# Part of the second-layer weights loaded from GpSimd's queue, in a one-core decode block

## The chip, the cores and the metric

The kernel runs on one core of a Trainium2 chip. The metric is the device time of one execution in microseconds (us), as a median of several runs. Five engines work beside each other: PE (TensorE, matmuls), DVE (VectorE), ACT (ScalarE), POOL (GpSimd) and SP (SyncE, which here only issues loads and the final store). Loads are carried by 16 DMA engines that all queues share.

## The reference

Two sequences (B = 2) of one token each pass an attention block with a cache and a dense block, both behind a layer norm. All data is float32.

```python
B, Sq, D = 2, 1, 512          # H, Sk, Dh = 32, 8192, 128 ; F = 1792
q = (layernorm(x) @ wq).reshape(B, Sq, H, Dh)
scores = einsum("bhqd,bhkd->bhqk", q, k_cache) * Dh ** -0.5
o = einsum("bhqk,bhkd->bhqd", softmax(scores), v_cache)
h = x + o.reshape(B, Sq, H * Dh) @ wo
r = relu(layernorm(h) @ w1 + b1)
out = h + (r * r) @ w2 + b2
```

The two caches are 64 pairs (head, sequence) of 4 MB of keys and 4 MB of values, 537 MB in all; the weights make up the rest of 561 MB.

## The kernel before

SBUF holds a ring of three slots of 64 KB per partition, `ring[0]` to `ring[2]`. One slot takes one pair: keys in its first half, values in its second. SP issues one load of 128 rows x 64 KB per pair (`load`, L127) whenever DVE has told it through the semaphore FREE that a slot is done; the loads run ahead of the work by up to two slots.

For each pair PE multiplies the keys with the query (L243), DVE takes the maximum (L249), ACT the exponential and its sum (L253), and DVE multiplies the values with the weights and sums (L258). Partial maxima, sums and products are kept and folded at the end.

The last pair is split up so that the end overlaps with its loads, and the slots are filled with the weights of the following layers. SP issues, in this order: the last keys (`kld`, slot 0), the first 24 heads of the output projection (`wod`, slot 1), the last values in three pieces (`vld`), the other 8 heads of `wod`, and, when slot 2 is free, the first-layer weights in two pieces (`w1d`) and the second-layer weights in four pieces (`w2d`, blocks 8, 4, 1 and 1 of the 14 blocks of 512 columns). Each load has a semaphore of its own that rises by 16 when all its parts have landed.

The compute at the end follows the same order. PE runs the output projection (L338) as its weights arrive, ACT and DVE form the second layer norm, PE multiplies with the first-layer weights (L386), DVE transposes, scales, adds the bias and squares the positive part (L396 to L403), and PE multiplies with the second-layer weights block by block (L410), waiting for each piece by `p.take(pe, LW2[k], 16)`. DVE copies the result (L415) and SP stores it (L417). Each block of L410 takes four matmuls in the code, which the trace shows as eight.

GpSimd builds an identity matrix at the start (L163, L165) and has nothing to do after that. The helper `p.take(engine, sem, n)` (L62) waits until a semaphore has reached n and takes n off again.

Of the kernel before, what the change touches and what calls it, by code (L numbers as in the profile page):

```python
# [17 lines left out]
FB = F // P  # L18
# [5 lines left out]
ROW = 2 * HALF  # L24
NG = BH - B
HG = H - 1
W2_PIECES = [8, 4, 1, 1]
W1_PIECES = [2, 2]
V_PIECES = [(0, 3), (3, 6), (6, 8)]
HA = 24  # L30
# [34 lines left out]
def attention_block_kernel(nc, small, kvd, wqd, kld, vld, wod, w1d, w2d, out):  # L65
    p = Program(nc)
    pe, dve, act, pool, sp = nc.tensor, nc.vector, nc.scalar, nc.gpsimd, nc.sync
# [52 lines left out]
    LV = [p.sem(f"v63_{k}") for k in range(len(V_PIECES))]  # L120
    LW1 = [p.sem(f"w1_{k}") for k in range(len(W1_PIECES))]
    LW2 = [p.sem(f"w2_{k}") for k in range(len(W2_PIECES))]
    FREE, SCORES, MAXED, EXPED, BUFFER, QUERY = (p.sem(n) for n in ("free", "scores", "maxed", "exped", "buffer", "query"))
    OUT = nc.alloc_semaphore("out")

    def load(tile, src, sem):
        sp.dma_start(tile, src).then_inc(sem, 16)  # L127

    W1 = ring[2][:, : DB * F].rearrange("p (d f) -> p d f", f=F)
    W2 = ring[2][:, DB * F : DB * F + FB * D].rearrange("p (m c) -> p m c", c=D)  # L130
# [19 lines left out]
        load(ring[0][:, HALF + a * CS : HALF + b * CS], vld[:, a * CS : b * CS], LV[k])  # L150
    load(WO[:, HA:], wod[:, HA:], LO)
    p.take(sp, FREE)
    at = 0
    for k, n in enumerate(W1_PIECES):
        load(W1[:, at : at + n], w1d[:, at : at + n], LW1[k])
        at += n
    at = 0
    for k, n in enumerate(W2_PIECES):
        load(W2[:, at : at + n], w2d[:, at : at + n], LW2[k])
        at += n  # L160
# [3 lines left out]
    p.after("pool", t_id)  # L164
    t_id = p.tell("pool", pool.affine_select(out=ident, in_=ident, compare_op=ALU.not_equal, fill=1.0, base=0,  # L165
                                             pattern=[[-1, P]], channel_multiplier=1))
    dve.memset(ones_d, 1.0 / D)
    dve.memset(eps_t, EPS)
    dve.memset(zero, 0.0)
# [232 lines left out]
    p.after("dve", tok)  # L402
    tok = p.tell("dve", dve.scalar_tensor_tensor(a2, a1, 0.0, a1, op0=ALU.max, op1=ALU.mult))  # L403
    p.after("pe", tok)
    at_m = 0
    for k, n in enumerate(W2_PIECES):
        p.take(pe, LW2[k], 16)
        for m in range(at_m, at_m + n):
            for j in range(NQ):
                ins = pe.matmul(o[32 * j : 32 * j + B, :], a2[:, m, :], W2[:, m, j * P : (j + 1) * P],  # L410
                                start=False, stop=(m == FB - 1))
        at_m += n
# [39 lines left out]
```

## Time and profile before

| | us |
|---|---|
| median of 3 runs | 1303.91 |
| lowest, highest | 1303.83, 1304.21 |
| the profiled execution's own time | 1303.67 |
| its span in the profile | 1301.9 |
| busy: PE, DVE, ACT, POOL | 412.5, 757.7, 160.1, 0.7 |

The profile comes from one execution. Its span runs from the first instruction to the end of the last one or of the last transfer; the 1.8 us beside it lie outside what the profile shows. A row of the timeline gives the start, the length, the engine, the line, the operation and its tiles, the count, and in brackets the idle time before it with the instruction that ended it. SPq and POOLq are the instruction queues of these engines. A row of the issues gives the tile and its source, the queue, the size and the time from issue to landing. The mean granted TensorE clock of this run was 0.637 of full speed.

### The profile page before, as it was taken

Reading aid. Unit: us, or ns where it says so; the run is one execution under the profiler, and the core shown is the slowest. Engines: PE = TensorE matmul, PEld = TensorE weight load, DVE = VectorE, ACT = ScalarE, POOL = GpSimd, SP = SyncE. Lnnn points to the kernel's source line nnn. Section 1 sums busy time; section 2 is a strip of 40 time slices with the busy share of each in tenths; the row PEclk is TensorE's granted clock in tenths of the full one; section 3 lists DMA queues with packets and bytes.
Section 4 is the critical chain, followed back from the end, with each engine's and each line's share of the span. In section 5 each row is a group of like instructions: output and inputs, shape, how many; then the busy total and the mean of one; then the engine's idle time right before and its main releaser. Section 6 shows DMA issues by size and latency. Waiting matters only on the chain. (4 is left out here: it accounts for less than half of the span.)

```text
span 1301.9 us, 8206 instructions
## 1 busy us (share of the span) xinstructions
PE 412.5 (32%) x2372; PEld 109.2 (8%) x2372; DVE 757.7 (58%) x1221; ACT 160.1 (12%) x267; POOL 0.7 (0%) x6
## 2 busy tenths in 40 slices
PE   1323223223323313323323323322322332331346
PEld 0100000000000000000000000000000000000012
DVE  1465575575565565566566466557557556556664
ACT  0011011011011011111111111101101101101120
POOL 0000000000000000000000000000000000000000
PEclk9766566666566566656656566656656666656668
DMA  9999999999999999999999999999999999999998
GB/s 419 419 448 423 445 423 447 423 441 429 421 449 421 447 423 445 423 447 423 443 427 423 447 421 447 423 447 421 447 423 445 425 429 441 421 447 423 447 412 368
DMA packets 11236, 561.13 MB, mean 431 GB/s; under 512 B 1376, under 2 KB 1504, under 8 KB 1760
## 3 DMA queue, kind: packets, MB, share of 16 engines
q1 hardware_dynamic: 11088, 561.06, 99.7%
q8 instruction: 3, 0.05, 0.0%
q10 hardware_dynamic: 144, 0.01, 0.0%
q14 instruction: 1, 0.01, 0.0%
HBM read 561.00 MB, written 0.07 MB: 431 GB/s over the span
## 5 line engine op out<-in xcount | busy, mean ns | idle before, releaser
L243 PE MATMUL s<-ring,qc 128*32 128x512 f32 x2048 | 376.8, 903 | 845.2 <-PEq L62 845.2
L258 DVE SCALAR_TENSOR_TENSOR ring<-ring,s 128x1024 f32<-128x1024 f32 x512 | 589.2, 1217 | 0.2 <-DVEq L62 0.2
L249 DVE TENSOR_REDUCE nm<-s 128x1024 f32 (+1 forms) x128 | 156.7, 1225 | 488.6 <-DVEq L62 488.6
L253 ACT ACTIVATE s<-s,nm 128x1024 f32<-128x1024 f32 x128 | 139.3, 1088 | 1081.6 <-ACTq L62 1081.6
L243 PEld LDWEIGHTS s<-ring,qc 128*32 128x32 f32 x2048 | 94.1, 157 | 1128.0 <-issue 1128.0
L258 DVE DVE_READ_ACCUMULATOR ring<-ring,s (+1 forms) x512 | 42.9, 84 | 0.0
L253 ACT ACTIVATION_READ_ACCUMULATOR s<-s,nm (+1 forms) x128 | 24.7, 193 | 0.0
L200 DVE TENSOR_REDUCE part<-sm 128x2 f32<-128x8 f32 x1 | 0.2, 161 | 19.4 <-DVEq L62 19.4
L338 PE MATMUL pm<-ring,big 128*32 128x512 f32 x64 | 10.7, 828 | 2.2 <-issue 1.4
L220 PE MATMUL s<-ring,xr 128*32 128x512 f32 x64 | 9.6, 770 | 2.3 <-issue 2.3
L202 PE MATMUL pm<-part,ones_d 128*128 128x2 f32 x2 | 0.6, 364 | 23.5 <-DVE part L200 23.5
L225 DVE STREAM_TRANSPOSE big<-s 128x512 f32<-128x512 f32 x2 | 1.4, 717 | 9.1 <-PE s L220 9.1
L274 DVE COPY qc<-qs 128x96 f32 x21 | 5.1, 243 | 0.0
L386 PE MATMUL s<-ring,xr 128*32 128x448 f32 x32 | 4.8, 726 | 0.5 <-issue 0.5
L193 ACT ACT_TABLE_LOAD x1 | 1.3, 1283 | 25.4 <-PE pm L191 25.4
L410 PE MATMUL s<-ring,a 128*2 128x128 f32 x112 | 3.5, 272 | 2.6 <-PEq L62 2.6
L372 DVE TENSOR_TENSOR hc<-xc,pm 128x8 f32<-128x8 f32 x1 | 0.2, 164 | 6.0 <-PE pm L366 6.0
L195 DVE RECIPROCAL rstd<-rstd 128x2 f32<-128x2 f32 x2 | 0.3, 166 | 5.5 <-ACT rstd L193 5.5
L220 PEld LDWEIGHTS s<-ring,xr 128*32 128x32 f32 x64 | 2.6, 137 | 8.4 <-issue 8.4
L338 PEld LDWEIGHTS pm<-ring,big 128*32 128x32 f32 x64 | 2.6, 143 | 8.2 <-issue 8.2
L297 PE MATMUL pm<-nm,pick 128*128 128x128 f32 x8 | 2.1, 441 | 3.7 <-DVE xb L290 3.7
L415 DVE COPY res<-s 128x128 f32<-128x128 f32 x1 | 0.3, 292 | 5.0 <-PE s L410 5.0
(62 smaller groups left out, 31.2 us busy)
## 6 DMA issues: line engine op xcount, KB each, us to landing
ring<-in_wod SPq DMA_DIRECT2D x1, 6144.0 KB, 27.3
ring<-in_kld SPq DMA_DIRECT2D x1, 4096.0 KB, 31.0
ring<-in_w1d SPq DMA_DIRECT2D x2, 1792.0 KB, 28.2
ring<-in_vld SPq DMA_DIRECT2D x2, 1536.0 KB, 32.2
ring<-in_wod SPq DMA_DIRECT2D x1, 2048.0 KB, 40.2
ring<-in_w2d SPq DMA_DIRECT2D x1, 2048.0 KB, 34.6
ring<-in_vld SPq DMA_DIRECT2D x1, 1024.0 KB, 35.8
ring<-in_w2d SPq DMA_DIRECT2D x1, 1024.0 KB, 36.7
```

Of the source, the lines that this page charges most:

```text
L193: tok = p.tell("act", act.activation(rstd, bank[:, :B], AF.Sqrt, bias=eps_t, scale=1.0))
L220: ins = pe.matmul(s[0][32 * j : 32 * j + 32, n * 512 : n * 512 + 512], xs[:, d, :], ring[2][:, c0 : c0 + 512], start=(d == 0), stop=(d == ...
L225: tok = p.tell("dve", dve.transpose(big[:, n * 512 : n * 512 + 512], s[0][:, n * 512 : n * 512 + 512]))
L243: ins = pe.matmul(s[k][32 * j : 32 * j + 32, n * 512 : (n + 1) * 512], qc[:, u, :], slot[:, c0 : c0 + 512], start=True, stop=True)
L249: dve.tensor_reduce(at(nm, pair, NC, c, 1), s[k], axis=AX.X, op=ALU.max, negate=True).then_inc(MAXED, 1)
L253: act.activation(s[k], s[k], AF.Exp, bias=at(nm, pair, NC, c, 1), scale=1.0, accum_out=at(ls, pair, NC, c, 1)).then_inc(EXPED, 1)
L258: return dve.scalar_tensor_tensor(v, v, 1.0, s[k], op0=ALU.mult, op1=ALU.mult, accum_out=at(ac, pair, NC * NH, c * NH + e, 1))
L274: dve.tensor_copy(qc, qs[:, bass.ds(i + 3, 3)][:, :, None].to_broadcast([P, 3, 32])).then_inc(QUERY, 1)
L297: ins = pe.matmul(pm[0][:, j * BH * NC : (j + 1) * BH * NC], pick[:, j, :], nm, start=True, stop=True)
L338: ins = pe.matmul(pm[1][32 * j : 32 * j + 32, :], big[:, h * 32 : h * 32 + 32], WO[:, h, :], start=(h < NQ), stop=(h + NQ >= H))
L386: ins = pe.matmul(y[32 * j : 32 * j + 32, :], xs[:, d, :], W1[:, d, j * FQ : (j + 1) * FQ], start=(d == 0), stop=(d == DB - 1))
L410: ins = pe.matmul(o[32 * j : 32 * j + B, :], a2[:, m, :], W2[:, m, j * P : (j + 1) * P], start=False, stop=(m == FB - 1))
```

## The change

The first two of the 14 blocks of `w2d` (4 KB in each of 128 partitions, 512 KB) are no longer part of SP's first second-layer load, which shrinks from 8 blocks to 6. GpSimd loads them in four loads that split the partitions into 12, 2, 98 and 16 rows. SP tells GpSimd through a new semaphore GO that slot 2 is free, right before it issues the first-layer weights. GpSimd waits for its four loads, resets its own record of DMA semaphores (`dma_reset`) and raises FIRST. PE waits for FIRST ahead of the first second-layer matmul.

```diff
-W2_PIECES = [8, 4, 1, 1]
+W2_PIECES = [6, 4, 1, 1]
+W2_FIRST = FB - sum(W2_PIECES)
+W2_ROWS = [12, 2, 98, 16]
...
     p.take(sp, FREE)
+    sp.sem_inc(GO, 1)
     at = 0
     for k, n in enumerate(W1_PIECES):
         load(W1[:, at : at + n], w1d[:, at : at + n], LW1[k])
         at += n
-    at = 0
+    at = W2_FIRST
     for k, n in enumerate(W2_PIECES):
         load(W2[:, at : at + n], w2d[:, at : at + n], LW2[k])
         at += n
...
+    p.take(pool, GO)
+    at = 0
+    for n, sem in zip(W2_ROWS, LW2F):
+        pool.dma_start(W2[at : at + n, :W2_FIRST], w2d[at : at + n, :W2_FIRST]).then_inc(sem, 16)
+        at += n
+    for sem in LW2F:
+        pool.wait_ge(sem, 16)
+    pool.dma_reset()
+    pool.sem_inc(FIRST, 1)
...
     p.after("pe", tok)
+    p.take(pe, FIRST)
     at_m = 0
     for k, n in enumerate(W2_PIECES):
         p.take(pe, LW2[k], 16)
+        n += W2_FIRST * (k == 0)
         for m in range(at_m, at_m + n):
```

More of the change, by code (lines that the diff above doesn't have):

```diff
@@ L122, in attention_block_kernel @@
     LW2 = [p.sem(f"w2_{k}") for k in range(len(W2_PIECES))]
+    LW2F = [p.sem(f"w2_rows_{k}") for k in range(len(W2_ROWS))]
+    GO, FIRST = p.sem("slot2"), p.sem("w2_first")
     FREE, SCORES, MAXED, EXPED, BUFFER, QUERY = (p.sem(n) for n in ("free", "scores", "maxed", "exped", "buffer", "query"))
```

## The prediction

> **What bounds the kernel now.** I read the page's head, its queue part and the stretches first, to see whether any engine sets the time.
>
> ```profile
> span 1301.9 us, 8206 instructions
> q1 hardware_dynamic: 11088, 561.06, 99.7%
> HBM read 561.00 MB, written 0.07 MB: 431 GB/s over the span
> ...
> 120.00:1200.00 1080.00, 330.51 (x1792) 82.46 (x1792) 649.86 (x1024) 134.91 (x224) 0.00 (x0) 0.62 1.00 434
> ```
>
> The first column group of the last row is the stretch, then busy us of PE, PEld, DVE, ACT and POOL, the granted TensorE clock, the share of the 16 DMA engines and GB/s. Through the body the DMA share is 1.00 at 434 GB/s, and DVE, the busiest engine, has work for 650 of 1080 us. The kernel is bound by its loads. 434 GB/s over 16 engines is 27.1 GB/s each, so a row of 4096 bytes (two blocks of 512 floats, what the change moves per partition) takes one engine 4096 / 27,100 = 0.151 us. Bytes are the same before and after, so nothing can come from the body; what is left is how the loads end. Next the end, in quarters of a microsecond:
>
> ```profile
> 1296.50:1297.00 0.50, 0.50 (x28) 0.50 (x20) 0.00 (x0) 0.00 (x0) 0.00 (x0) 1.00 0.98 369
> 1297.00:1297.25 0.25, 0.25 (x17) 0.25 (x12) 0.00 (x0) 0.00 (x0) 0.00 (x0) 1.00 1.04 393
> 1297.25:1297.50 0.25, 0.25 (x20) 0.22 (x8) 0.00 (x0) 0.00 (x0) 0.00 (x0) 1.00 0.57 213
> 1297.50:1297.75 0.25, 0.25 (x12) 0.00 (x0) 0.00 (x0) 0.00 (x0) 0.00 (x0) 1.00 0.50 148
> 1297.75:1298.00 0.25, 0.01 (x2) 0.00 (x0) 0.00 (x0) 0.00 (x0) 0.00 (x0) 1.00 0.23 90
> 1298.00:1298.25 0.25, 0.00 (x0) 0.00 (x0) 0.00 (x0) 0.00 (x0) 0.00 (x0) 1.00 0.19 74
> 1298.25:1298.50 0.25, 0.15 (x8) 0.18 (x12) 0.00 (x0) 0.00 (x0) 0.00 (x0) 1.00 0.13 49
> 1298.50:1298.75 0.25, 0.25 (x16) 0.25 (x12) 0.00 (x0) 0.00 (x0) 0.00 (x0) 1.00 0.13 49
> 1298.75:1299.00 0.25, 0.25 (x16) 0.25 (x12) 0.00 (x0) 0.00 (x0) 0.00 (x0) 1.00 0.11 41
> 1299.00:1299.25 0.25, 0.25 (x20) 0.25 (x13) 0.00 (x0) 0.00 (x0) 0.00 (x0) 1.00 0.00 0
> ```
>
> This is the view that matters. A share of 0.13 is two engines of 16. All sixteen are busy until 1297.25; about twelve run dry around 1297.4; one more by 1298.0 (0.23 is under four), a third laggard by about 1298.25 (0.19 is three), and the last two work alone from 1298.25 to 1299.0. Every load of 128 rows is dealt over all engines, so each of its semaphores waits for the last of them. From 1297.25 on the column of GB/s gives (213+148+90+74+49+49+41) x 0.25 = 166 KB, which sixteen engines would move in 0.38 us: perfect balance would end the loads at 1297.63 instead of 1299.0. **So 1.4 us is the most that any redistribution can gain**, about 0.1% of the time.
>
> Why there are laggards: instruction packets of 16 KB go through single DMA engines beside the loads.
>
> ```profile
> q8 instruction: 2, 0.03, 0.3%
> ```
>
> That is the queue row of 1250 to 1302 us: two such packets, 0.6 us of one engine each at 27.1 GB/s. Whoever carries one is late for good, since its queue of loads never runs empty to catch up.
>
> Last, what PE does with the loads at the end:
>
> ```profile
> 1282.36 3.45 PE L338 MATMUL pm<-ring,big 128*32 128x512 f32 x16 [0.87 <-PEq L62]
> 1288.36 2.75 PE L386 MATMUL s<-ring,xr 128*32 128x448 f32 x16 [0.48 <-issue]
> 1291.56 2.06 PE L386 MATMUL s<-ring,xr 128*32 128x448 f32 x16
> 1294.82 0.19 DVE L403 SCALAR_TENSOR_TENSOR a<-a 128x28 f32<-128x28 f32 x1
> 1295.83 1.93 PE L410 MATMUL s<-ring,a 128*2 128x128 f32 x64 [2.00 <-PEq L62]
> 1298.35 1.62 PE L410 MATMUL s<-ring,a 128*2 128x128 f32 x48 [0.59 <-PEq L62]
> 1299.54 0.14 PEld L410 LDWEIGHTS s<-ring,a 128*2 128x2 f32 x8 [0.21 <-issue]
> 1300.04 0.29 DVE L415 COPY res<-s 128x128 f32<-128x128 f32 x1 [5.03 <-PE s L410]
> 1300.35 0.34 SPq L417 DMA_DIRECT2D out<-res  x1
> ...
> 1242.01 0.43 SPq L127 DMA_DIRECT2D ring<-in_wod  x1
> 1260.23 0.80 SPq L127 DMA_DIRECT2D ring<-in_w1d  x2
> 1261.08 8.84 SPq L127 DMA_DIRECT2D ring<-in_w2d  x4
> ...
> ring<-in_w1d SPq DMA_DIRECT2D x2, 1792.0 KB, 28.2
> ring<-in_wod SPq DMA_DIRECT2D x1, 2048.0 KB, 40.2
> ring<-in_w2d SPq DMA_DIRECT2D x1, 2048.0 KB, 34.6
> ```
>
> The second-layer matmuls (L410) stop and start with the loads: the activations are ready when L403 ends at 1295.01, but PE starts at 1295.83, since the first eight blocks land at 1261.1 + 34.6 = 1295.7; it stops again at 1297.76 for the next four, and the last eight weight loads begin at 1299.54, 0.54 after the last data packet. The copy, the store and the end follow at fixed distances. The other boundary is 1282.36: L338 starts right behind the second part of the output projection's weights, 1242.0 + 40.2 = 1282.2, and from there to L403 the chain is latency of compute.
>
> **The change, part by part.** Removed from SP: nothing but bytes, 8 blocks become 6 in one load; the four issues remain. Added to SP: one increment ahead of the first-layer loads; SP's next row is an issue that lands 28 us later, so it costs nothing. Added to PE: one wait (FIRST) ahead of L410, beside a wait that is 0.8 us longer; nothing but those matmuls is queued behind it. Added to POOL: a wait, four issues, four waits, a reset, an increment. POOL has nothing behind them and nobody waits for it except through FIRST.
>
> *When the rows land.* GpSimd's DMA issues are not in this trace. The nearest rows for a second queue beside SP's are those of the start:
>
> ```profile
> sm<-in_small ACTq DMA_DIRECT2D x1, 13.0 KB, 22.4
> ring<-in_wqd SPq DMA_DIRECT2D x1, 22.2
> ```
>
> 13 KB took as long as the load of 64 KB rows issued beside it: 8 small rows per engine took turns, one for one, with 8 big ones of 2.4 us (65,536 / 27,100). So here 9 or 10 rows take turns with what SP has queued when POOL is told, at 1260.23: rows of 48 KB (1.8 us) at worst. Ten rounds and four semaphore packets of 1.8 us end by 1286 with an issue time near SP's 0.4; on rows of 8 to 16 KB (0.3 to 0.6 us), which follow soon, nearer 1273. Both lie ahead of 1295.0, so FIRST is expected open, for nothing. The cover is 9 us in the worse case and over 20 in the likelier.
>
> *What they delay.* The moved rows come ahead of loads that were queued before them. An engine that carries 8 of them is 1.21 us later with the projection's weights, one with 9 is 1.36, one that is spared 0.15. From the first-layer loads' end on, the moved bytes are missing from SP's first second-layer load and the schedule is back.
>
> *Who carries what.* Eight rows per engine before. 12 + 2 + 98 + 16 is dealt anew: 98 is 14 x 7, so two engines get none of it, which saves them up to 7 x 0.151 = 1.06 us against eight rows, if one row of the 16 is left to them. With shares of one row for the 12, the 2 and the 16, counted from the first engine each time, the loads are 10, 10, ten times 9, 8, 8, 1, 1. The trace doesn't number the engines. Between the ends (the spared two are the last two: -1.06 for them; they are not: +0.15 to +0.30) I take the first, narrowly, because there are exactly two engines far behind. The Trainium skill, "DMA: Bandwidth & Descriptors", section on why a DMA increments its semaphore by 16, gives both dealings: k engines with k dividing the rows, from a cursor that moves on, or, for some direct copies from GpSimd, shares rounded up over all sixteen. By the second the two spared are the last-numbered; by the first the spared two depend on the cursor and get 2 rows, and 0.15 us less is saved. No run here shows which it is.
>
> *The sum, if the last two are spared.* Their end goes from 1299.0 to 1297.94. The twelve go from about 1297.4 to 1297.7 at most. What is late next is the third laggard, at 1298.25 with eight rows, unchanged. So the loads end 0.75 us earlier. PE must follow: the projection's weights now wait for that third engine, which was 0.75 ahead and is 1.21 later, +0.46; L403 ends at 1295.5 and L410 starts at 1295.6, its first piece having landed at 1295.7 - 0.75. Its 112 matmuls need 1.93 + 1.62 - 0.21 = 3.34 and would be through at 1298.9; the last piece, landing 0.75 earlier, lets the last eight weight loads begin at 1298.8 and the copy at 1299.3. Both agree, with little to spare. The copy comes 0.7 us earlier. The profiled execution took 1303.67, its span 1301.9 and 1.8 around it; the median of 1303.91 stands 0.24 above it. 1303.91 - 0.7 = **1303.2 us**.
>
> **The rivals.**
>
> *The spared engines are not the laggards.* Then the last two carry 9 or 10 rows and end 0.15 to 0.30 later; the projection's weights come 1.4 later, L403 ends at 1296.4, and PE's 3.34 us end at 1299.8, just inside. Copy at 1300.2 to 1300.3: 1303.91 + 0.2 = 1304.1 us. For it: 14 of 16 engines are not those two. Against it: nothing in the trace.
>
> *Nothing changes.* If GpSimd's queue deals 98 rows nearly evenly (98 / 16 is 6.1), or spares one laggard and not the other, the end stays: 1303.9 us. The Trainium skill, same page, section "Issuing engines are not separate DMA queues", speaks for this: all queues end on the same 16 engines, and issuing from several saves only issue time. By that rule the sum is 0. The body's 434 GB/s at a share of 1.00 agrees with it, but the quarters above show a loss that is balance and not rate.
>
> *The gate comes late (slower).* If GpSimd's rows queue behind what SP has already issued, they land with or after the last loads, and PE holds all 112 matmuls back at FIRST. PE then needs 3.34 us after the last landing where it now needs 0.5: 1303.91 + 2.9 = 1306.8 us. It decides from FIRST open later than about 1296.6 (1299.97 - 3.34), each microsecond costing one. For it: the backlog is 28 to 35 us at issue, as the times to landing say. Against it: the small load of the start, which took turns.
>
> **How the numbers follow.** Last two spared 0.50 (1303.2); others spared 0.30 (1304.1); nothing 0.09 (1303.9); gate late 0.06 (1306.8); 0.03 for another cost of the new queue that passes 2.6 us, 0.02 for a gain that passes it, which the 1.4 us above all but excludes. 0.2% of the time, 2.6 us, is about what a measurement of this kernel can tell from no change; the first three cases lie inside. Faster 0.02, same 0.89, slower 0.09. The range takes in the first three, with 0.4 below the first for a third laggard that also gains a little and 0.5 above the second for the issue costs not seen: 1302.8 to 1304.6.
>
> **What would show it.** Right: the DMA share falls from 1.0 to nothing within about 0.8 us instead of 1.75; L410 starts near 1295.6 and runs with hardly a stop; the copy comes 0.7 us earlier; POOL's rows land before 1286; L338's second start moves to about 1282.8. Wrong: two engines still alone for 0.75 us (others spared), L338's second start at 1283.6 (same), L410 waiting for FIRST past 1296.6 (gate late), or a span that is unchanged with a longer time around it.

## The result, and the profile after

The changed kernel takes 1307.59 us (13 runs, 1305.77 to 1308.08) where the kernel before takes 1303.91 (13 runs, 1303.65 to 1304.48). The ratio is 1.0025 with a 95% interval of 1.0017 to 1.0032: 3.7 us slower. The runs before lie in one group, those after in two, 1305.8 to 1306.2 and 1307.1 to 1308.1. The profiled execution of after took 1307.60, that of before 1303.67, so 3.93 us are to be explained between the two.

The page of after, and its issues and queue rows from 1250 us on. GpSimd's queue is q0.

```profile
span 1305.9 us, 8216 instructions
q1 hardware_dynamic: 11088, 560.53, 99.4%
q0 software_dynamic: 224, 0.52, 0.1%
...
ring<-in_w2d POOLq DMA_DIRECT2D x1, 392.0 KB, 13.0
ring<-in_w2d POOLq DMA_DIRECT2D x1, 64.0 KB, 13.5
ring<-in_w2d POOLq DMA_DIRECT2D x1, 48.0 KB, 7.5
ring<-in_w2d POOLq DMA_DIRECT2D x1, 8.0 KB, 7.4
ring<-in_wod SPq DMA_DIRECT2D x1, 2048.0 KB, 42.8
```

Rows from the end of the timeline of after (L131 issues a load, L175 GpSimd's, L272 is the product with the values, L352 the output projection, L417 the end of the activations, L426 the second-layer matmuls, L431 the copy).

```profile
1242.93 0.43 SPq L131 DMA_DIRECT2D ring<-in_wod  x1
1260.18 2.23 POOL L175 DMA_DIRECT2D ring<-in_w2d  x4 [1258.71 <-POOLq L64]
1274.33 1.22 DVE L272 SCALAR_TENSOR_TENSOR ring<-ring,s 128x1024 f32<-128x1024 f32 x1 [3.78 <-DVEq L64]
1283.06 1.22 DVE L272 SCALAR_TENSOR_TENSOR ring<-ring,s 128x1024 f32<-128x1024 f32 x1
1285.87 3.64 PE L352 MATMUL pm<-ring,big 128*32 128x512 f32 x16 [0.83 <-PEq L64]
1300.22 0.19 DVE L417 SCALAR_TENSOR_TENSOR a<-a 128x28 f32<-128x28 f32 x1
1300.66 3.24 PE L426 MATMUL s<-ring,a 128*2 128x128 f32 x112 [1.44 <-PEq L64]
1303.97 0.29 DVE L431 COPY res<-s 128x128 f32<-128x128 f32 x1 [3.56 <-PE s L426]
```

The two rows of before that answer to the products:

```profile
1271.30 1.22 DVE L258 SCALAR_TENSOR_TENSOR ring<-ring,s 128x1024 f32<-128x1024 f32 x1
1279.56 1.22 DVE L258 SCALAR_TENSOR_TENSOR ring<-ring,s 128x1024 f32<-128x1024 f32 x1
```

The gate does no harm: the rows land 7 to 14 us after their issues, by 1276. The loss begins with the values. DVE now waits 3.78 us for their first piece and starts at 1274.33 instead of 1271.30; its last product starts 3.50 later, and the second half of the projection 3.51 later (1282.36 to 1285.87). Its weights are as late as its products: they land at 1242.9 + 42.8 = 1285.7. From there to the end of the activations it takes 14.54 us instead of 12.65, another 1.89. Part comes back: PE waits 0.25 us instead of 0.82 for the second layer, and from its first matmul to the copy it takes 3.31 instead of 4.21, since no load stops it any more. 3.51 + 1.89 - 0.57 - 0.90 = 3.93.

Where the 3.5 us come from shows in the stretch in which GpSimd's rows move, 1264 to 1276 us. The last two columns are the DMA engines' busy share and GB/s. Before:

```profile
1264.00:1276.00 12.00, 7.24 (x45) 3.30 (x48) 8.49 (x14) 2.15 (x6) 0.00 (x0) 0.53 0.94 394
```

After:

```profile
1264.00:1276.00 12.00, 7.23 (x50) 2.76 (x53) 5.64 (x10) 1.96 (x4) 0.00 (x0) 0.58 0.92 306
```

The engines are nearly as busy (0.92 against 0.94) and move 22% less. (394 - 306) GB/s x 12 us is 1.06 MB, or 2.4 us of all sixteen at 434 GB/s. That is not a matter of who waits for whom but of rate.

And the end of the loads after, to be held against the quarters of the prediction:

```profile
1298.00:1298.50 0.50, 0.50 (x12) 0.16 (x8) 0.00 (x0) 0.00 (x0) 0.00 (x0) 1.00 0.98 393
1298.50:1299.00 0.50, 0.50 (x16) 0.15 (x8) 0.00 (x0) 0.00 (x0) 0.00 (x0) 1.00 0.89 344
1299.00:1299.25 0.25, 0.23 (x12) 0.00 (x0) 0.16 (x1) 0.00 (x0) 0.00 (x0) 1.00 0.95 369
1299.25:1299.50 0.25, 0.00 (x0) 0.00 (x0) 0.25 (x1) 0.00 (x0) 0.00 (x0) 1.00 0.98 385
1299.50:1299.75 0.25, 0.00 (x0) 0.00 (x0) 0.24 (x1) 0.00 (x0) 0.00 (x0) 1.00 0.67 254
...
1300.25:1300.50 0.25, 0.00 (x0) 0.00 (x0) 0.16 (x1) 0.00 (x0) 0.00 (x0) 1.00 0.19 74
1300.50:1300.75 0.25, 0.09 (x4) 0.12 (x8) 0.00 (x0) 0.00 (x0) 0.00 (x0) 1.00 0.19 74
1300.75:1301.00 0.25, 0.25 (x14) 0.24 (x15) 0.00 (x0) 0.00 (x0) 0.00 (x0) 1.00 0.17 66
1301.00:1301.25 0.25, 0.25 (x20) 0.25 (x12) 0.00 (x0) 0.00 (x0) 0.00 (x0) 1.00 0.07 25
1301.25:1301.50 0.25, 0.25 (x20) 0.25 (x12) 0.00 (x0) 0.00 (x0) 0.00 (x0) 1.00 0.02 8
```

About three engines (0.19, 0.17) still work alone from 1300.25 to 1301.0, and one (0.07, 0.02) until about 1301.3, where before two worked until 1299.0: the laggards are still there and the loads end 2.3 us later.

### The profile page after: what moved, and what is told of

The parts are those of the page before. It is cut to its first block, busy times and chain, and to the rows that moved or that the text cites. A ratio compares the mean times of both kernels' runs of the same rounds, so it can differ in the third digit from the quotient of the medians.

```text
span 1305.9 us, 8216 instructions
## 1 busy us (share of the span) xinstructions
PE 399.7 (31%) x2372; PEld 107.9 (8%) x2372; DVE 757.9 (58%) x1221; ACT 160.0 (12%) x267; POOL 2.9 (0%) x10
## 5 line engine op out<-in xcount | busy, mean ns | idle before, releaser
L257 PE MATMUL s<-ring,qc 128*32 128x512 f32 x2048 | 363.1, 873 | 858.6 <-PEq L64 858.6
L272 DVE SCALAR_TENSOR_TENSOR ring<-ring,s 128x1024 f32<-128x1024 f32 x512 | 589.3, 1217 | 4.4 <-DVEq L64 4.4
L272 DVE DVE_READ_ACCUMULATOR ring<-ring,s (+1 forms) x512 | 42.8, 84 | 0.0
L352 PE MATMUL pm<-ring,big 128*32 128x512 f32 x64 | 10.7, 824 | 2.2 <-issue 1.4
L175 POOL DMA_DIRECT2D ring<-in_w2d x4 | 2.2, 565 | 1258.7 <-POOLq L64 1258.7
L426 PE MATMUL s<-ring,a 128*2 128x128 f32 x112 | 3.2, 272 | 1.4 <-PEq L64 1.4
## 6 DMA issues: line engine op xcount, KB each, us to landing
ring<-in_wod SPq DMA_DIRECT2D x1, 2048.0 KB, 42.8
```

Source lines behind the costliest of these rows:

```text
L175: pool.dma_start(W2[at : at + n, :W2_FIRST], w2d[at : at + n, :W2_FIRST]).then_inc(sem, 16)
L257: ins = pe.matmul(s[k][32 * j : 32 * j + 32, n * 512 : (n + 1) * 512], qc[:, u, :], slot[:, c0 : c0 + 512], start=True, stop=True)
L272: return dve.scalar_tensor_tensor(v, v, 1.0, s[k], op0=ALU.mult, op1=ALU.mult, accum_out=at(ac, pair, NC * NH, c * NH + e, 1))
L352: ins = pe.matmul(pm[1][32 * j : 32 * j + 32, :], big[:, h * 32 : h * 32 + 32], WO[:, h, :], start=(h < NQ), stop=(h + NQ >= H))
```

## The experiments

My theory after reading the two traces was that the dealing of the rows costs the rate: a load of 128 rows gives each engine always the same partitions, while loads of 12, 2, 98 and 16 rows put partitions on engines that serve others (theory D). The rivals: the queue that GpSimd writes is slow for the engines (S), or any second queue beside SP's is (Q).

**e1, one load of 128 rows on GpSimd.**

```diff
-W2_ROWS = [12, 2, 98, 16]
+W2_ROWS = [128]
```

> Edit: GpSimd loads the same 512 KB in one load of 128 rows instead of 12, 2, 98 and 16. While GpSimd's rows moved in the changed kernel (1264 to 1274 us), the DMA engines were as busy as before but moved 300 to 340 GB/s where 418 to 430 was moved before. Theory D (the dealing: uneven shares put rows on engines that otherwise serve other partitions, and those transfers get in each other's way): with 128 rows dealt by eights the rate stays near 420, the first values (V, first piece) are awaited until about 1272 instead of 1274.3, the time is 1303.7 to 1304.5. Theory S (the software queue itself slows the engines): rate 300 to 340 again, time 1306 to 1308. Theory Q (any second queue): like S.

Measured: 1303.76 us (10 runs, 1303.43 to 1305.64), ratio to before 1.0001, 0.9991 to 1.0010. Its stretch, first product and second half of the projection:

```profile
1264.00:1276.00 12.00, 7.24 (x40) 3.52 (x42) 7.48 (x13) 2.65 (x6) 0.00 (x0) 0.50 0.93 387
...
1272.39 1.22 DVE L272 SCALAR_TENSOR_TENSOR ring<-ring,s 128x1024 f32<-128x1024 f32 x1 [0.62 <-DVEq L64]
1283.55 3.44 PE L352 MATMUL pm<-ring,big 128*32 128x512 f32 x16 [0.94 <-PEq L64]
```

The rate is back, on the same queue, for the same bytes at the same time. The moved bytes alone delay the first product by 1.09 us and the projection by 1.19; the median hides that, though three of the ten runs took 1305.4 to 1305.6. Theory S falls.

**e2 and e3, the same rows and the one load of 128 rows on ACT's queue.**

```diff
-    p.take(pool, GO)
...
+    p.take(act, GO)
+    r0 = 0
+    for n, sem in zip(W2_ROWS, LW2F):
+        act.dma_start(W2[r0 : r0 + n, :W2_FIRST], w2d[r0 : r0 + n, :W2_FIRST]).then_inc(sem, 16)
+        r0 += n
...
-    p.take(pe, FIRST)
+    for sem in LW2F:
+        p.take(pe, sem, 16)
```

> Edit: the four loads of 12, 2, 98 and 16 rows are issued by ACT, at the same signal from SP; PE waits for their four semaphores itself; nothing is left on GpSimd. Theory D: rate falls to 300 to 340 GB/s as in the changed kernel, time 1306 to 1308. Theory S: rate near 420 and time 1303.5 to 1304.5. Theory Q: like D.

> Edit: as the ACT kernel, but one load of 128 rows. Theory D and theory S: rate near 420, time 1303.5 to 1304.5. Theory Q (two queues taking turns cost a quarter of the rate, whoever issues): rate 300 to 340 and time 1306 to 1308.

Measured: e2 1308.37 us (7 runs, 1306.66 to 1310.06), ratio 1.0032, 1.0020 to 1.0043; e3 1303.93 (10 runs, 1303.61 to 1305.89), ratio 1.0004, 0.9995 to 1.0014. e2 lies 0.4 us above the 1306 to 1308 expected of it; why was not followed up. The stretch in e2:

```profile
1264.00:1276.00 12.00, 7.24 (x50) 2.71 (x52) 4.88 (x8) 1.96 (x4) 0.00 (x0) 0.58 0.90 309
...
q10 hardware_dynamic: 172, 0.52, 2.6%
```

In e3:

```profile
1264.00:1276.00 12.00, 8.07 (x56) 3.06 (x60) 6.72 (x12) 1.97 (x4) 0.00 (x0) 0.61 0.91 379
```

The loss goes with the rows and not with the queue: 309 GB/s with 12, 2, 98 and 16 rows, 379 with 128. Theory Q falls too.

**e4, GpSimd's rows signalled after all of SP's issues.**

```diff
-    sp.sem_inc(GO, 1)
...
     for k, n in enumerate(W2_PIECES):
         load(W2[:, at : at + n], w2d[:, at : at + n], LW2[k])
         at += n
+    sp.sem_inc(GO, 1)
```

> Edit: as the changed kernel, but SP signals GpSimd after its four second-layer issues (near 1270 us) instead of ahead of the first-layer issues (1259.6). GpSimd's rows then come among the first-layer weights and no longer among the last values. If the place does the harm (the values' first piece 3 us late, then the chain of products): DVE's products start by 1271.5 and end by 1281, and the time is set by the last load, 1303.5 to 1306.5 according to how much rate is lost there (up to 2.4 us). If the rate alone does it, wherever it falls: 1306 to 1308.

Measured: 1307.29 us (10 runs, 1305.85 to 1308.23), ratio 1.0024, 1.0014 to 1.0034, as slow as the changed kernel. Its rows:

```profile
1276.00:1280.00 4.00, 3.05 (x32) 0.67 (x20) 3.36 (x7) 0.00 (x0) 0.00 (x0) 1.00 1.01 338
1280.00:1284.00 4.00, 0.24 (x8) 0.16 (x8) 1.92 (x7) 0.00 (x0) 0.00 (x0) 0.83 1.06 325
...
1271.43 1.21 DVE L272 SCALAR_TENSOR_TENSOR ring<-ring,s 128x1024 f32<-128x1024 f32 x1
1286.24 3.52 PE L352 MATMUL pm<-ring,big 128*32 128x512 f32 x16 [4.14 <-PEq L64]
```

The values are on time now, at 1271.43, but the dip has moved with the rows, to 1276 to 1284 us, and the projection's second half waits 4.14 us for its weights instead. Of the two places tried neither is free: the values wait for loads in one, the projection in the other, and the time is as long.

**e5, e6 and e7, what in the dealing does it.** Other engines than those of a 128-row load (D1 below), or only unequal shares, 1 to 10 rows per engine (D2)? The three edits, all on GpSimd:

```diff
-W2_ROWS = [12, 2, 98, 16]
+W2_ROWS = [32, 32, 32, 32]        # e5
+W2_ROWS = [64, 64]                # e7
...
-        pool.dma_start(W2[at : at + n, :W2_FIRST], w2d[at : at + n, :W2_FIRST]).then_inc(sem, 16)
+        c = slice(256 * (n % 2), 256 * (n % 2) + 256)                       # e6, n = 0 to 3
+        pool.dma_start(W2[:, n // 2, c], w2d[:, n // 2, c]).then_inc(sem, 16)
```

> Edit: GpSimd's four loads have 32 rows each instead of 12, 2, 98 and 16, so that every engine carries the same 8 rows in all, but two at a time and of partitions it doesn't serve in a load of 128 rows. Theory D1 (rows dealt to other engines than the 128-row loads use for those partitions): 300 to 340 GB/s or less while they move, first product (V) at 1274 or later, time 1306.5 to 1309. Theory D2 (only the unequal shares, 1 to 10 rows per engine): rate near 420, first product by 1272.5, time 1303.5 to 1305.9.

> Edit: GpSimd loads the same 512 KB in four loads of all 128 rows, each 1 KB per row (half a block), so four loads with their semaphores as in the changed kernel, but the dealing of a 128-row load. Theories D1 and D2: rate near 420, time 1303.5 to 1305.9. If the number of loads or of semaphore packets did it: rate 300 to 340 and 1306 to 1308.

> Edit: GpSimd's loads are two of 64 rows each, 4 rows per engine at a time, equal in sum. Theory D1: part of the engines meet the partitions of others, so slower than the one load of 128 rows: rate 300 to 400, time 1305 to 1308. Theory D2: as the load of 128 rows, 1303.5 to 1305.9.

Measured: e5 1306.97 us (10 runs, 1305.89 to 1307.95), ratio 1.0022, 1.0013 to 1.0032; e6 1304.12 (10 runs, 1303.68 to 1305.78), ratio 1.0002, 0.9993 to 1.0012; e7 1307.09 (10 runs, 1306.05 to 1308.15), ratio 1.0024, 1.0014 to 1.0033. The stretch in e5, four loads of 32 rows:

```profile
1264.00:1276.00 12.00, 7.24 (x49) 3.16 (x51) 4.85 (x8) 1.99 (x5) 0.00 (x0) 0.55 0.92 309
```

In e6, four loads of 128 rows:

```profile
1264.00:1276.00 12.00, 7.23 (x48) 2.85 (x50) 7.40 (x12) 1.96 (x4) 0.00 (x0) 0.57 0.92 376
```

In e7, two loads of 64 rows:

```profile
1264.00:1276.00 12.00, 7.23 (x48) 2.92 (x50) 4.85 (x8) 1.96 (x4) 0.00 (x0) 0.57 0.93 303
```

Loads of 32 and of 64 rows divide evenly over sixteen engines, eight each in all, as in a load of 128, and the loss is whole. Four loads with four times the semaphores, but of 128 rows, lose nothing that the median shows. So it isn't the unequal shares and isn't the number of loads; what e5, e7 and the change have in common is loads of fewer than 128 rows.

**e8, the same rows without a second queue.** SP issues them itself, behind the first-layer weights; GpSimd's part is left out.

```diff
-    at = W2_FIRST
+    at = 0
+    for n, sem in zip(W2_ROWS, LW2F):
+        load(W2[at : at + n, :W2_FIRST], w2d[at : at + n, :W2_FIRST], sem)
+        at += n
+    at = W2_FIRST
...
-    p.take(pe, FIRST)
+    for sem in LW2F:
+        p.take(pe, sem, 16)
```

> Edit: SP itself issues the four loads of 12, 2, 98 and 16 rows, in its one queue behind the first-layer weights; no GpSimd, no second queue. Theory D1: the rows still meet the partitions of engines that are at other rows, the rate dips where they move and the loads end later: 1304.5 to 1306.5, less than the changed kernel as nothing queued ahead is delayed. If two queues are needed for the loss: 1303.5 to 1304.5.

Measured: 1306.62 us (10 runs, 1305.83 to 1307.62), ratio 1.0020, 1.0010 to 1.0029, just above what I expected. Its rows:

```profile
1284.00:1288.00 4.00, 3.20 (x19) 1.02 (x12) 0.00 (x0) 0.69 (x2) 0.00 (x0) 0.73 1.02 434
1288.00:1292.00 4.00, 3.52 (x23) 1.44 (x22) 0.85 (x5) 0.00 (x0) 0.00 (x0) 0.70 1.01 253
1292.00:1296.00 4.00, 2.90 (x17) 0.93 (x21) 0.17 (x1) 0.26 (x1) 0.00 (x0) 0.50 1.00 336
```

The dip comes where the rows are in SP's own queue, down to 253 GB/s at a busy share of 1.01. So neither GpSimd nor a second queue is needed for the loss.

**e9 to e11, the changed kernel three times more**, one execution each, for the other 1.9 us: the chain of compute from the projection's second half to the end of the activations.

> The changed kernel once more, for its profile. So far its executions lie in two groups, 1305.8 to 1306.2 and 1307.1 to 1308.1 us. Theory C (the granted TensorE clock in the chain from the projection's second half to the activations): 12.6 to 12.8 us at a mean clock near 0.74 where the time is about 1306, 14.4 to 14.8 us near 0.58 where it is about 1307.7, the loads alike in both. Rival L (the loads differ): the chain is equally long and the projection's second half starts at different times.

> As the one before: time about 1306 with a chain of 12.6 to 12.8 us near 0.74, or about 1307.7 with 14.4 to 14.8 us near 0.58 (theory C); or the difference lies in the start of the projection's second half (rival L).

> As the two before: time about 1306 with a chain of 12.6 to 12.8 us near 0.74, or about 1307.7 with 14.4 to 14.8 us near 0.58 (theory C); or the difference lies in the start of the projection's second half (rival L).

Measured: 1305.98, 1305.96 and 1305.90 us, all of the lower group. Of e9:

```profile
1285.85 3.39 PE L352 MATMUL pm<-ring,big 128*32 128x512 f32 x16 [0.82 <-PEq L64]
1298.24 0.19 DVE L417 SCALAR_TENSOR_TENSOR a<-a 128x28 f32<-128x28 f32 x1
1302.36 0.29 DVE L431 COPY res<-s 128x128 f32<-128x128 f32 x1 [3.93 <-PE s L426]
...
1285.90:1298.60 12.70, 10.08 (x68) 3.54 (x68) 2.22 (x10) 0.95 (x3) 0.00 (x0) 0.75 1.00 419
```

The same stretch of after, from the projection's second half to the end of the activations:

```profile
1285.87:1300.41 14.54, 12.13 (x68) 4.76 (x68) 2.23 (x10) 0.95 (x3) 0.00 (x0) 0.58 0.95 398
```

In before:

```profile
1282.36:1295.01 12.65, 10.19 (x68) 3.61 (x68) 2.23 (x10) 0.95 (x3) 0.00 (x0) 0.74 0.99 420
```

In e2, e5 and e7, whose profiled executions took 1308.37, 1307.95 and 1308.04 us:

```profile
1286.15:1300.50 14.35, 11.95 (x68) 4.76 (x68) 2.23 (x10) 0.95 (x3) 0.00 (x0) 0.59 0.95 399
1285.93:1300.76 14.83, 12.43 (x68) 4.84 (x68) 2.23 (x10) 0.95 (x3) 0.00 (x0) 0.57 0.93 389
1286.19:1300.68 14.49, 12.09 (x68) 4.75 (x68) 2.23 (x10) 0.95 (x3) 0.00 (x0) 0.59 0.96 399
```

And in e6, the shortest of all:

```profile
1283.80:1295.47 11.67, 8.87 (x68) 3.40 (x68) 2.23 (x10) 0.95 (x3) 0.00 (x0) 0.82 0.99 419
```

The projection's second half starts at 1285.85 in e9 and at 1285.87 in after, the loads end at about 1301.3 in both, and the rate of the stretch from 1264 to 1276 is 309 and 306 GB/s: the loads are alike. DVE and ACT do the same 2.2 and 0.95 us of work. What differs is PE, with the granted clock (third column from the right): its 68 matmuls are busy for 8.9 us at 0.82, for 10.1 to 10.2 near 0.74 and for 12.1 at 0.58. In the trace of after the clock stays at 0.50 in one piece from 1281 to 1298 us, while in that of e9 it is back at 1.00 from 1288.9 to 1292.2. The copies lie 1.61 us apart, the times 1.62. That is what theory C expected, and rival L falls. The upper group rests on one trace of this kernel, with those of e2, e5 and e7 beside it, and why the clock differs from one execution to the next stays open.

## Why the prediction was wrong

**The step that failed is the price of a row.** "What they delay" and "Who carries what" charged 0.151 us per row of 4 KB to the engine that carries it, at the body's 434 GB/s, whichever engine that is. For a load of 128 rows that price holds: eight rows make 1.21 us, and e1 measured 1.19 for the projection (e3 and e6 1.36 and 1.44); e1's loads end at 1299.0, as in before. For loads of fewer rows it does not: they take the rate of all sixteen engines from 394 to 306 GB/s over the 12 us in which they move, which is 2.4 us of all engines, against the 1.4 us that the best balance could have gained. None of my rivals had it, beyond the 0.03 kept for another cost of the new queue: I took the rate from a body made of 128-row loads only, and gave all of the doubt to which engines would be spared. The row for it was missing in the trace of before, which has no load of other than 128 rows, and there I should have kept a bound on the rate itself.

**The term "+0.46", or 1.4 among the rivals**, for the projection's second half measured +3.51. Of that, e1's 1.19 is the moved bytes; the rest, 2.3, is the lost rate.

**That two engines would be spared, and that they were the laggards, did not show.** The share falls to 0.89 at 1298.5, but is back at 0.98 just before the end, and about three engines are still alone after it. Nor is it shown that instruction packets make the laggards: of the two in before one began at 1274.9 and the other at 1297.6, when the share had already begun to fall. How the rows are dealt can now be counted, though. Beside its rows a queue carries semaphore packets, each of which raises a load's semaphore. GpSimd's queue has 224 packets: 128 rows and 4 x 16 semaphores leave 32, which is what loads of 12, 2, 98 and 16 rows need to fill 16, 16, 16 x 7 and 16 places (160 - 128). In e5, e6 and e7, whose rows divide by sixteen, none are left over (192, 192 and 160 packets). That fits shares rounded up over all sixteen, as I took them: 10, 10, ten times 9, 8, 8, 1, 1; which engine got which share the trace does not say. ACT's queue in e2 has 172 packets: 128 rows and 44, which is 12 + 2 + 14 + 16: one semaphore packet for each engine used, the number of engines dividing the rows. These are the two rules that the Trainium skill gives in "DMA: Bandwidth & Descriptors", in the section "Why a DMA increments its semaphore by 16 and not by 1"; the traces agree with the rounded-up shares for GpSimd and with the dividing number for ACT. Both dealings cost the same rate (306 and 309 GB/s).

**PE's chain was taken as fixed.** The 12.65 us from the projection to the activations hold at a granted clock of 0.74 only. In before a slower chain would be mostly hidden, since PE waits 0.82 us for the second-layer weights and is stopped by their pieces again: my estimate for 1.89 us more is 1295.01 + 1.89 + 3.34 = 1300.24, beside a copy that now starts at 1300.04. No trace of before has a slow chain, so this is not shown. In after nothing hides it. So 2.3 us of the loss are the loads (1305.98 against 1303.67; they end 2.3 later), and by the trace of after another 1.6 come with the clock; 10 of its 13 executions lie in that group. A few executions of the 128-row kernels are late as well (three of ten in e1 and in e3, one in e6, at 1305.4 to 1305.9); a slow chain would account for them, but none of these was traced.

**What held.** The rows took turns with SP's, landed by 1276 (1273 to 1286 predicted), and PE started 0.25 us after the activations, so FIRST held nothing up: the slower rival's mechanism did not occur, and that the time came out near its 1306.8 is chance. GpSimd's issues cost 2.23 us for four and nobody waited for them. PE's 112 matmuls took 3.24 us, 3.34 predicted, and ran without a stop. The time around the span stayed (1.7 us, 1.8 before).

## What to carry to other kernels

Where the loads are the bound, load all 128 partitions at a time and split along the columns if a load must be split: e6's four loads of 128 rows cost nothing in the median, e7's two halves of 64 rows 3.2 us. The waits show only where a loss is felt; here the busy share stayed and the rate fell, and bytes divided by time in the stretch showed it. And before trading slack at the end against balance, ask what the slack was hiding, here a chain whose length follows the granted clock.

## What the runs showed of the hardware

Loads of 2 to 98 rows beside full traffic take the sixteen DMA engines from 376 to 387 GB/s (loads of 128 rows, same bytes) down to 303 to 314 over 12 us, on GpSimd's queue and on ACT's, and to 253 over 4 us in SP's own. The Trainium skill, "DMA: Bandwidth & Descriptors", section "The descriptor swizzle", says that in a 128-partition load each engine writes its own eight partitions, at one port of SBUF. My inference is that loads of fewer rows, dealt in other shares, send several engines to one port. The traces agree with it in that 128 rows are fast and 64, 32 and the mixed rows are not; they don't number the engines or the ports, so the collision itself is not shown, nor whether it would be on the side of SBUF or of HBM, where the same rows are read in another order.

The same 68 matmuls took PE from 8.9 to 12.1 us at mean granted clocks from 0.82 to 0.58, and put executions of one kernel 1.6 us apart.
